# A list schedule's table refitted to corrected durations, with the first q load in two pieces

## The chip, the cores and the metric

The kernel runs on one core of one Trainium2 chip. The metric is the device time of one execution in microseconds, taken as the median of several runs. The engines are named as in the profile: PE multiplies matrices, PEld loads its weights, DVE and ACT work elementwise on 128 partitions, SP issues DMAs, POOL does almost nothing here. ACT issues a few DMAs too (its queue is written ACTq, that of SP is SPq).

## What is computed

Three stages in a row, all in float32. Attention with a threshold (4 batches, 8 heads, 576 positions, head size 64), then a feed-forward layer with softmax and layer norm (2304 tokens, 512 to 1024 to 512), then one with softplus (512 to 2048 to 512):

```python
scores = scale * np.matmul(q, k.transpose(0, 1, 3, 2))
thresh = np.max(scores, axis=-1, keepdims=True) - tau
scores = np.where(scores >= thresh, scores, -1000000000.0)
attn = softmax(scores)            # written out in full in the reference
x = np.matmul(attn, v)            # heads side by side: 2304 x 512
...
h = x @ w_in
solu = h * softmax(h)
ln = (solu - mean(solu)) / np.sqrt(var(solu) + 1e-06) * g_ln
x = ln @ w_out
...
h = x @ w2_in
g = np.maximum(h, 0.0) + np.log1p(np.exp(-np.abs(h)))
out = g @ w2_out
```

## The kernel before

The program is straight-line code: every instruction is written out once. What stands where is decided when the kernel is built, by `Plan`. Each piece of work is an `Op` with an engine, a time that it holds its engine (`occ`), a time until others can use its result (`fin`), what it comes after, what buffers it takes, and a due number. `Plan.order` plays the program through: at each step it takes the engine that can start soonest and on it the ready operation with the least due number. The order that comes out is then emitted, engine by engine, and is fixed; on the chip each engine works through its own list in order and waits on semaphores. The due numbers come from the tables at the top of the file (`JT`, `JA`, `LO`, `LAGS`, `LD`, `JIT`, `PREP` and single numbers), which were fitted. So a wrong duration in an `Op` costs nothing by itself; it gives an order that doesn't suit the chip.

Attention is cut into 44 items, numbered as `n` below. An item is one pair of heads with one or two tiles of 128 queries (or the last 64 queries of two pairs: a tail item, `T`). For each tile PE makes the scores (`s`, line 393; of tail items line 450), DVE takes the maximum (line 349), ACT the exponential (350), DVE masks and sums (352), then come the reciprocals (357, 358) and their spreading (402, 408, 410), PE transposes the weights (368), ACT copies them to SBUF (371), and PE multiplies with v (429). The scores of the next tile need both score buffers back, and these come free with the two exponentials.

Beside this run the weights of the first layer: w_in and w_out come as 64-bit words and are turned into pairs of float32 (ACT 488, DVE 489, 491, 492, then ACT 503 or 500 and DVE 501 or PE 512/513 with ACT 515). The first layer's matmuls on a unit of 256 tokens (line 567; its softmax and norm in lines 584 to 598, its transposes in 610, its second matmul in 627 and 628) are put between the attention work. The second layer (lines 678 and 701) follows; its w_out is loaded and converted in 16 chunks when the first layer has given back its memory: two chunks have been loaded by then, and the third (`raw_out2`) waits for the buffer of the first.

Where the plan sees PE idle for long early in the program it puts filler matmuls there (line 288), which compute nothing that is used.

Of the kernel before, what the change touches and what calls it, by code (L numbers as in the profile page):

```python
# [39 lines left out]
LD = [-11.06, 0.35, 9.2, 14.07, 7.04, 12.77, 7.9, 34.61, 19.66, 38.52, 7.77, 68.68, 10.48, 84.79, 20.67, 17.31, 4.65, 8.82, 1.55, -62.61, -15.71, -19.93, 81.02, 16.74, 91.83, 70.72, 19.84, -5.66, -48.3, 4.79, -22.69, -44.85]  # L40
JIT = [-11.99, -8.79, -5.19, -5.48, 1.8, -10.03, 0.87, -8.03, 6.15, -0.57, 3.09, -24.47, 0.08, 2.59, -34.82, 4.62, 7.64, 16.92, 9.09, 3.38, -14.37, -6.4, -10.15, 3.76, -6.77, -11.43, -14.53, -18.35, -5.02, -26.2, -15.19, -13.01, -2.79, 0.51, -17.2, 8.63, -5.03, -12.19, -11.44, -4.71, -8.08, -1.06, -14.31, -9.49]
YLAG = 4.72
PLOAD = -16.03
W2IN = 60.61
W2OUT = -5.81
TURNED = 4
STICK = 0.48
PREP = [-18.8, -45.68, -12.55, 12.05, 71.4, 119.39, -150.07, 43.1]


def f(ap):
    return ap.bitcast(F32)
# [27 lines left out]
WARM = 130e3  # L80

# [7 lines left out]
class Plan:  # L89
# [17 lines left out]
    def order(self):  # L107
# [12 lines left out]
        mode, dma, done = "", 0, []  # L120
        win, work, slow = 0, {}, False
# [31 lines left out]
        while any(cand.values()):  # L153
# [110 lines left out]
def plan_of(nc, ctx, sb, const, ident, minus, pools, stacks, w1t, x2s, q, k, v, tau, w_in, w_out, g_ln, w2_in, w2_out, out):  # L264
# [5 lines left out]
    plan = Plan(dict(w=W_, s=S_, h2=4, E=NE, T=2, eT=NET, x=2, xr=NXR, xrT=1, q=NPAIR, k=NPAIR, v=NPAIR, ln=3, u=2,  # L270
# [3 lines left out]
    def buf(pool, tag, name, shape, dtype=F32, bufs=1):  # L274
        return Buf(pool, tag, lambda: pools[pool].tile(shape, dtype, tag=tag, name=name, bufs=bufs))
# [23 lines left out]
    o_minus = op("ACT", 200, 300, lambda: act.activation(out=minus, in_=ident, func=AF.Copy, scale=-1.0), after=[o_ident], due=-60)  # L299
    o_table = op("ACT", 1300, 1300, lambda: act.preload_act_table_set("natural_log_exp_and_others"), due=-49.5)  # L300

    def queue(what, i):
        return "ACT" if f"{what}{i}" in ON_ACT else "SP"

    def load_qk(p, due):
# [4 lines left out]
        z["kq"], ql = [], []  # L310
# [3 lines left out]
        for h in range(2):  # L314
            r = slice(64 * h, 64 * h + 64)
            ql.append(load(queue("q", p), lambda r=r: q_.t[r, :], lambda h=h: q[p][:, 640 * h:640 * h + 576], 144, takes=() if h else [q_], uses=[q_] if h else (), due=due))
        z["scaled"] = op("ACT", 574, 678, lambda: act.activation(out=q_.t, in_=q_.t, func=AF.Copy, scale=0.125), after=ql, uses=[q_], due=due + 0.5)
# [37 lines left out]
    def inverse(n, w, sums, masks, due):  # L355
        rv = buf("at", "rinv", f"rinv{n}", [P, 4], bufs=4)
# [20 lines left out]
    def item(n):  # L377
# [4 lines left out]
        sums = buf("at", "sums", f"sums{n}", [P, 4], bufs=4)  # L382
        E = [buf("at", "E", f"E{n}_{i}", [P, 1152], bufs=NE) for i in range(nt)]
        masks = {}
        for kk, i in enumerate(ts):
# [8 lines left out]
            sc = op("PE", 970, 1128, emit_s, after=z["kq"] + [z["scaled"]], takes=s, uses=[z["q"], z["k"]], due=j + JIT[n], mode="R")  # L394
# [7 lines left out]
        o3 = op("ACT", 187 if nt == 1 else 310, 298 if nt == 1 else 410, lambda: act.copy(out=rb.t[:, 0:w, :], in_=rv.t[:, 0:w].unsqueeze(2).to_broadcast([P, w, 64])), after=[o2], takes=[rb], uses=[rv], due=jl + D_SUM)  # L402
# [7 lines left out]
        xc = op("ACT", 162 if nt == 1 else 263, 270 if nt == 1 else 395, lambda: act.copy(out=x.t[:, 0:W], in_=rbk.t[:, 0:W]), after=[rg], uses=[rbk, x], due=jl + D_X)  # L410
# [25 lines left out]
    def tail_item(n):  # L436
# [424 lines left out]
```

## Time and profile before

| what | value |
|---|---|
| median of 3 runs | 912.28 us (912.16 to 912.69) |
| the profiled execution | 914.37 us |
| its span, first to last instruction | 912.6 us |
| PE busy, share of the span | 899.6 us, 99% |
| DVE busy | 690.4 us, 76% |
| ACT busy | 591.1 us, 65% |
| mean granted clock of PE | 0.996 |

The profiled execution took 2.1 us more than the median, and 1.8 us of it lies outside its span. A busy PE is not a PE at its peak, since its matmuls overlap: what can be read is where it is idle, where it runs filler, and the pace from one matmul's start to the next.

### The profile page before, as it was taken

How to read it: one execution, taken by the hardware profiler on the slowest of the kernel's cores; microseconds unless marked ns; L12 is line 12 of the kernel's file. 1: busy time of each engine (PE TensorE's matmuls, PEld its weight loads, DVE VectorE, ACT ScalarE, POOL GpSimd, SP SyncE). 2: the span in 40 equal slices, each digit the busy share in tenths (PEclk: the TensorE clock that was granted, in tenths of full speed). 3: DMA queues.
4: the chain of work that ended last, by engine and by line, in shares of the span. 5: the costliest groups of instructions: out<-in, count | busy, mean ns of one | idle time of the engine just before them, and what ended most of it. 6: DMA issues, size and time to landing. Idle time of an engine off the chain costs nothing.

```text
span 912.6 us, 14433 instructions
## 1 busy us (share of the span) xinstructions
PE 899.6 (99%) x5458; PEld 709.6 (78%) x5458; DVE 690.4 (76%) x1474; ACT 591.1 (65%) x1159; POOL 0.7 (0%) x6
## 2 busy tenths in 40 slices
PE   8999999999999999999999999999999999999998
PEld 6576676677677677788888878888888888888897
DVE  5999898898777778599958969985556555655565
ACT  6978887997778687676757746764444444444454
POOL 0000000000000000000000000000000000000000
PEclk9999999999999999999999999999999999999999
DMA  9405110230231000164414223430021001100010
GB/s 281 161 1 175 54 30 1 84 83 24 66 109 62 2 1 12 59 219 162 139 59 162 93 98 110 135 119 24 1 92 47 1 1 47 47 0 1 1 47 24
DMA packets 32052, 64.63 MB, mean 71 GB/s; under 512 B 3440, under 2 KB 12912, under 8 KB 31984
## 3 DMA queue, kind: packets, MB, share of 16 engines
q1 hardware_dynamic: 31104, 61.62, 20.8%
q10 hardware_dynamic: 880, 2.10, 0.8%
q8 instruction: 43, 0.70, 0.3%
q14 instruction: 25, 0.20, 0.1%
HBM read 49.55 MB, written 14.16 MB: 70 GB/s over the span
## 4 chain that ended last, share of the span: by engine, by line
PE 83%; DVE 7%; ACT 4%; DMA 4%; issue 1%; SPq 1%; ACTq 0%; DVEq 0%
PE w L701 21%; PE h L678 20%; PE w L567 8%; PE w L368 7%; PE w L429 6%; PE s L393 6%; PE w L627 6%; PE w L628 3%; PE w L610 1%; PE w L472 1%; DMA raw<-in_w_in_dram 1%; DVE E L352 1%; DVE nm L349 1%; PE s L450 1%; DMA q<-in_q_dram 1%
## 5 line engine op out<-in xcount | busy, mean ns | idle before, releaser
L678 PE MATMUL h<-x2m,w2h 128*128 128x512 f32 (+1 forms) x640 | 181.6, 368 | 0.0
L678 PEld LDWEIGHTS h<-x2m,w2h 128*128 128x128 f32 x640 | 116.5, 188 | 21.0
L349 DVE TENSOR_REDUCE nm<-s 128x1 f32<-128x576 f32 x144 | 102.7, 752 | 21.7 <-PE s L393 19.1
L678 PE MATMUL h<-x2m,w2l 128*128 128x512 f32 (+1 forms) x320 | 117.7, 368 | 0.0
L701 PE MATMUL w<-wo2h,gh 128*128 128x512 f32 x288 | 112.9, 392 | 1.1 <-ACT wo2h L503 1.1
L701 PE MATMUL w<-wo2l,gh 128*128 128x512 f32 x288 | 113.0, 393 | 0.6 <-DVE wo2l L505 0.6
L352 DVE SCALAR_TENSOR_TENSOR E<-E,etau 128x576 f32<-128x576 f32 x128 | 101.1, 815 | 16.3 <-ACT E L350 14.9
L701 PE MATMUL w<-wo2h,gl 128*128 128x512 f32 x288 | 112.7, 391 | 0.0
L371 ACT COPY eT<-w 128x512 f32<-128x512 f32 (+1 forms) x188 | 92.9, 554 | 19.5 <-PE w L368 18.9
L689 ACT ACTIVATE t<-h 128x512 f32<-128x512 f32 (+1 forms) x80 | 44.3, 554 | 90.9 <-PE h L678 90.9
L627 PE MATMUL w<-lhl,wo1h 128*128 128x512 f32 x288 | 102.8, 397 | 0.0
L350 ACT ACTIVATE E<-s,nm 128x576 f32<-128x576 f32 x128 | 91.6, 756 | 11.2 <-DVE nm L349 11.0
L691 DVE TENSOR_SCALAR gw<-t 128x512 f32<-128x512 f32 (+1 forms) x80 | 31.8, 399 | 80.3 <-ACT t L690 80.1
L693 ACT ACTIVATE gw<-gw 128x512 f32<-128x512 f32 (+1 forms) x80 | 47.1, 589 | 61.1 <-DVE t L692 60.0
L393 PE MATMUL s<-k,q 64*128 64x288 f32 x512 | 83.9, 429 | 2.0 <-ACT E L350 1.4
L628 PE MATMUL w<-lhl,wo1l 128*128 128x256 f32 x288 | 80.7, 280 | 0.0
L429 PE MATMUL w<-eT,v 128*64 128x256 f32 (+1 forms) x720 | 77.8, 364 | 1.6 <-ACT eT L371 1.5
L368 PE MATMUL w<-ident,E 128*128 128x128 f32 x576 | 78.4, 279 | 0.0
L368 PEld LDWEIGHTS w<-ident,E 128*128 128x128 f32 x576 | 63.6, 141 | 17.4 <-issue 6.4
L694 DVE SCALAR_TENSOR_TENSOR gw<-h,gw 128x512 f32<-128x512 f32 (+1 forms) x80 | 51.0, 637 | 33.1 <-ACT gw L693 32.0
L429 PEld LDWEIGHTS w<-eT,v 128*64 128x64 f32 x720 | 47.1, 138 | 28.0 <-ACT eT L371 4.4
L678 PEld LDWEIGHTS h<-x2m,w2l 128*128 128x128 f32 x320 | 60.3, 188 | 10.1
(107 smaller groups left out, 1573.2 us busy)
## 6 DMA issues: line engine op xcount, KB each, us to landing
x2s<-x SPq DMA_DIRECT2D x36, 256.0 KB, 2.0
x2m<-x2s SPq DMA_DIRECT2D x18, 512.0 KB, 6.0
raw_in<-in_w_in_dram SPq DMA_DIRECT2D x16, 512.0 KB, 3.8
raw_out<-in_w_out_dram SPq DMA_DIRECT2D x16, 512.0 KB, 3.6
v<-in_v_dram SPq DMA_DIRECT2D x15, 320.0 KB, 3.4
q<-in_q_dram SPq DMA_DIRECT2D x28, 144.0 KB, 3.6
out_dram<-yo SPq DMA_DIRECT2D x15, 256.0 KB, 2.1
raw<-in_w_out_dram SPq DMA_DIRECT2D x3, 1024.0 KB, 7.8
```

Of the source, the lines that this page charges most:

```text
L349: mx = op("DVE", 668, 750, lambda: dve.tensor_reduce(out=nm.t, in_=src(), axis=AX.XY, op=ALU.max, negate=True), after=[after], takes=[nm], ...
L350: ex = op("ACT", 638, 741, lambda: act.activation(out=dst().rearrange("p (a b) -> p a b", a=2), in_=src(), func=AF.Exp, bias=nm.t, scale=1.0),
L352: return op("DVE", 739, 900, lambda: dve.scalar_tensor_tensor(out=dst(), in0=dst(), scalar=etau, in1=dst(), op0=ALU.is_ge, op1=ALU.mult, a ...
L368: pe.transpose(bk.t[:, P * i:P * i + P], b_.t[:, c:c + P], ident)
L371: copies.append(op("ACT", occ, occ + 111, lambda: act.copy(out=eT.t[:, 0:width], in_=bk.t[:, 0:width]), after=[g], uses=[bk, eT], due=due))
L393: pe.matmul(s[h].t[:, nh, 0:288], z["q"].t[r, c:c + P], z["k"].t[r, 288 * nh:288 * nh + 288], start=True, stop=True)
L429: pe.matmul(o_.t[64 * h:64 * h + 64, 0:W], z["v"].t[:, vcols(c, h)], e[8 if c == 8 else 4 * h + c](), start=(i == 0), stop=(i == 4))
L567: pe.matmul(ps.t, x__[:, part, :], w_[:, part, 512 * n:512 * n + 512], start=(part == 0 and j_ == 0), stop=(part == 3 and j_ == 2))
L627: pe.matmul(o.t.rearrange("p (a q) -> p a q", a=2), w1t["wo1h"][:, c, P * m:P * m + P], lhl.t[:, :, c, :], start=(c == 0), stop=False)
L628: pe.matmul(o.t[:, 0:256], w1t["wo1l"][:, c, P * m:P * m + P], lhl.t[:, 0, c, :], start=False, stop=(c == 7))
L678: pe.matmul(ps.t[:, 0:n], w2t["in", a, c][:, part, :], x.t[:, b_, part, 0:n], start=(part == 0 and j_ == 0), stop=(part == 3 and j_ == 2))
L701: pe.matmul(ys[j].t, g_.t[:, P * j:P * j + P], w2t["out", a, c], start=(c == 0 and i == 0), stop=(c == NC2 - 1 and i == 2))
```

## The change

Five things are changed. Durations of some operations are set anew: ACT's share of the conversions (lines 488, 500, 503), DVE's in line 501, the scaling of the tail items' rows (460, 461), the spreading copies (402, 410). The plan takes the first loads to land later (`FIRST`), and lets PE start at the low clock. The first q load is cut at column 192 of 576, with a scaling for each piece, and the second piece goes through SP. `sums` and `rinv` get eight buffers for four, and the plan is told that there is one `rb`. Two setup operations on ACT change places. Then all fitted tables are new.

```diff
-JT = [0.34, 7.73, 0.9, -3.39, 0.54, ...
+JT = [-0.31, 8.41, -0.42, -4.07, -3.04, ...
...
-AHEAD = dict(PE=0, DVE=0, ACT=0, SP=20, POOL=20, X=20)
+AHEAD = dict(PE=75, DVE=0, ACT=0, SP=35, POOL=20, X=20)
...
-STICK = 0.48
+STICK = 0.03
...
+FIRST = 2500
...
-        mode, dma, done = "", 0, []
-        win, work, slow = 0, {}, False
+        mode, dma, done = "", FIRST, []
+        win, work, slow = 0, {}, True
...
-    o_minus = op("ACT", 200, 300, lambda: act.activation(out=minus, in_=ident, func=AF.Copy, scale=-1.0), after=[o_ident], due=-60)
-    o_table = op("ACT", 1300, 1300, lambda: act.preload_act_table_set("natural_log_exp_and_others"), due=-49.5)
+    o_minus = op("ACT", 200, 300, lambda: act.activation(out=minus, in_=ident, func=AF.Copy, scale=-1.0), after=[o_ident], due=-5)
+    o_table = op("ACT", 1300, 1300, lambda: act.preload_act_table_set("natural_log_exp_and_others"), due=-80)
...
+        cuts = [0, 192, S] if p == 0 else [0, S]
+        z["scaled"] = []
+        for a, e in zip(cuts, cuts[1:]):
...
-        rv = buf("at", "rinv", f"rinv{n}", [P, 4], bufs=4)
+        rv = buf("at", "rinv", f"rinv{n}", [P, 4], bufs=8)
...
-            sc = op("PE", 970, 1128, emit_s, after=z["kq"] + [z["scaled"]], takes=s, uses=[z["q"], z["k"]], due=j + JIT[n], mode="R")
+            sc = op("PE", 970, 1128, emit_s, after=z["kq"] + z["scaled"][0:1 if i == 0 else 2], takes=s, uses=[z["q"], z["k"]], due=j + JIT[n], mode="R")
...
-            t2.append(op("ACT", 590, 695, lambda i=i: act.activation(...), after=[t1[i]], ...))
+            t2.append(op("ACT", 667, 765, lambda i=i: act.activation(...), after=[t1[i]], ...))
...
-        a1 = op("ACT", 100 + 950 * k_, 200 + 960 * k_, ...)
+        a1 = op("ACT", 69 + 1022 * k_, 181 + 1008 * k_, ...)
...
-                h = op("ACT", 525, 620, lambda i=i: act.activation(out=hi()[:, i, :], ...))
+                h = op("ACT", 666, 794, lambda i=i: act.activation(out=hi()[:, i, :], ...))
```

What the tables do to the order is seen in the built programs. Three places are shown, and in all of them the changed program's lines stand seven lower, as its file is longer. ACT at the very start, before the change (`q_101` is the first q, `q_132` the second, `E_0_168` the weights of item 0, `etau` needs the load of tau):

```order
L295 DMA q_101<-in_q_dram 64x576 x2
L299 ACT_TABLE_LOAD
L299 ACTIVATE minus<-ident 128x128
L300 ACT_TABLE_LOAD
L317 ACTIVATE q_101<-q_101 128x576
L734 ACTIVATE etau<-tau_sb 128x1
L317 ACTIVATE q_132<-q_132 128x576
L350 ACTIVATE E_0_168<-s_0_0_139,nm_0_148 128x576
L350 ACTIVATE E_0_168<-s_0_1_140,nm_1_164 128x576
```

And in the changed program (`q_120` is the first q, `q_129` the second):

```order
L301 ACT_TABLE_LOAD
L296 DMA q_120<-in_q_dram 64x192 x2
L300 ACTIVATE minus<-ident 128x128
L741 ACTIVATE etau<-tau_sb 128x1
L324 ACTIVATE q_120<-q_120 128x192
L324 ACTIVATE q_120<-q_120 128x384
L357 ACTIVATE E_0_165<-s_0_0_139,nm_0_148 128x576
L324 ACTIVATE q_129<-q_129 128x576
L357 ACTIVATE E_0_165<-s_0_1_140,nm_1_163 128x576
```

One table load is gone, the other stands ahead of the q load, `etau` ahead of the first scaling, and the scaling of the second q between the two exponentials of item 0. On SP the two DMAs of the first q's second piece stand fourth and fifth, behind k and tau, and the third and fourth k and q now come ahead of the second to fourth v.

PE from the scores of item 6 to those of item 7, before the change (`E4` and `E5` are weights of items 4 and 5):

```order
L393 MATMUL s6_0_0_493<-k2_145,q2_162 128x288
L368 MATMUL w30_503<-ident_81,E4_0_412 128x128 x4
L368 MATMUL w31_514<-ident_81,E4_0_412 128x128 x4
L368 MATMUL w32_521<-ident_81,E4_0_412 128x128
L368 MATMUL w35_524<-ident_81,E5_0_470 128x128 x4
L393 MATMUL s7_0_1_543<-k3_186,q3_203 128x288
```

And the last rows of the same stretch in the changed program:

```order
L436 MATMUL w33_534<-eT4_4_509,v0_137 64x128
L415 MATMUL w29_551<-ident_81,rb4_520 128x128
L375 MATMUL w35_554<-ident_81,E5_0_503 128x128 x4
L375 MATMUL w36_564<-ident_81,E5_0_503 128x128 x4
L375 MATMUL w37_572<-ident_81,E5_0_503 128x128
L519 MATMUL w7_578<-raw1_3_2_275,ident_81 128x512
L520 MATMUL w7_578<-w1h_83,minus_82 128x512
L400 MATMUL s7_0_1_588<-k3_171,q3_182 128x288
```

Between the scores of item 6 and the first of these rows stand eight more of line 436 (item 4's product with v). So item 4's product, ten transposes and a pair for the conversions now lie between the two scores, where thirteen transposes lay.

DVE at the third chunk of the second layer's w_out (`raw_out2`, ending in `wo2l2`), before the change:

```order
L489 TENSOR_SCALAR raw_out2_6385<-raw_out2_6385 128x512
L691 TENSOR_SCALAR gw0_5_6420<-t0_5_6256 128x512
L491 SCALAR_TENSOR_TENSOR raw_out2_6385<-raw_out2_6385 128x512
L489 TENSOR_SCALAR raw_out3_6391<-raw_out3_6391 128x512
L492 SCALAR_TENSOR_TENSOR raw_out2_6385<-raw_out2_6385 128x512
L491 SCALAR_TENSOR_TENSOR raw_out3_6391<-raw_out3_6391 128x512
L697 TENSOR_TENSOR gl0_4_6442<-gw0_4_6243,gh0_4_6432 128x512
L505 TENSOR_TENSOR wo2l2_6323<-raw_out2_6385,wo2h2_6322 128x512
```

And in the changed program:

```order
L496 TENSOR_SCALAR raw_out2_6396<-raw_out2_6396 128x512
L498 SCALAR_TENSOR_TENSOR raw_out2_6396<-raw_out2_6396 128x512
L499 SCALAR_TENSOR_TENSOR raw_out2_6396<-raw_out2_6396 128x512
L496 TENSOR_SCALAR raw_out3_6401<-raw_out3_6401 128x512
L704 TENSOR_TENSOR gl0_3_6439<-gw0_3_6206,gh0_3_6432 128x512
L498 SCALAR_TENSOR_TENSOR raw_out3_6401<-raw_out3_6401 128x512
L512 TENSOR_TENSOR wo2l2_6334<-raw_out2_6396,wo2h2_6333 128x512
```

The chunk's first three steps now follow each other with nothing between them.

## Rows read from the trace of the kernel before

**Rows 1.** Windows: us, busy of PE, PEld, DVE, ACT, POOL (instructions); clock, DMA.

```profile
0.00:25.52 25.52, 21.27 (x172) 17.31 (x172) 15.16 (x31) 17.49 (x32) 0.70 (x6) 1.00 0.94 295
25.52:49.90 24.38, 23.35 (x136) 14.98 (x134) 23.38 (x57) 23.01 (x47) 0.00 (x0) 0.93 0.29 105
49.90:97.90 48.00, 47.00 (x387) 33.48 (x387) 46.58 (x94) 39.44 (x77) 0.00 (x0) 1.00 0.28 84
97.90:120.40 22.50, 22.03 (x176) 15.22 (x175) 19.97 (x50) 20.60 (x44) 0.00 (x0) 1.00 0.26 71
120.40:157.40 37.00, 37.00 (x277) 25.24 (x277) 34.93 (x90) 29.95 (x63) 0.00 (x0) 1.00 0.03 9
157.40:347.50 190.10, 189.45 (x1573) 136.02 (x1571) 155.19 (x360) 149.38 (x305) 0.00 (x0) 1.00 0.17 52
533.90:547.32 13.42, 11.69 (x44) 8.95 (x43) 8.75 (x17) 4.57 (x8) 0.00 (x0) 0.87 0.37 122
```

**Rows 2.** Timeline of ACT and ACTq, first items: start, length, instruction, idle before.

```profile
0.74 1.49 ACTq L295 DMA_DIRECT2D q<-in_q_dram  x2
2.26 1.28 ACT L299 ACT_TABLE_LOAD   x1 [2.26 <-issue]
6.01 0.68 ACT L317 ACTIVATE q<-q 128x576 f32<-128x576 f32 x1 [0.84 <-DMA q<-in_q_dram]
8.77 0.68 ACT L317 ACTIVATE q<-q 128x576 f32<-128x576 f32 x1 [1.99 <-DMA q<-in_q_dram]
12.78 0.28 ACT L402 COPY rb<-rinv 128x128 f32<-128x128 f32 x1
17.23 0.69 ACT L317 ACTIVATE q<-q 128x576 f32<-128x576 f32 x1 [1.07 <-DMA q<-in_q_dram]
```

**Rows 3.** Timeline of SPq, and the landing of tau by tile.

```profile
2.00 0.59 SPq L295 DMA_DIRECT2D tau_sb<-in_tau_dram  x1
3.77 1.24 SPq L295 DMA_DIRECT2D q<-in_q_dram  x2
DMA to landing us min/median/max: 4.1/4.1/4.1
```

**Rows 4.** Timeline of PE, the start.

```profile
1.35 4.92 PE L288 MATMUL w<-ident 128*128 128x128 f32 x28 [1.35 <-POOL ident masks.py:199]
6.74 1.31 PE L393 MATMUL s<-k,q 64*128 64x288 f32 x8 [0.47 <-ACT q L317]
```

**Rows 5.** Timeline of PE around the scores of item 7.

```profile
40.65 1.64 PE L368 MATMUL w<-ident,E 128*128 128x128 f32 x13
43.29 1.87 PE L393 MATMUL s<-k,q 64*128 64x288 f32 x8 [1.00 <-ACT E L350]
```

**Rows 6.** Windows around the two stretches at half clock.

```profile
42.14:45.56 3.42, 2.42 (x15) 1.33 (x15) 3.42 (x11) 3.42 (x9) 0.00 (x0) 1.00 0.00 0
45.56:48.97 3.41, 3.41 (x27) 3.08 (x24) 2.52 (x8) 2.46 (x7) 0.00 (x0) 0.50 0.00 0
543.90:547.32 3.42, 3.42 (x9) 2.65 (x10) 3.42 (x7) 1.45 (x3) 0.00 (x0) 0.50 0.56 169
```

**Rows 7.** The chain that ended last: a run of first-layer matmuls.

```profile
334.80 2.75 PE w L567 x12
```

**Rows 8.** Timeline of PE: transposes between matmuls, and the third chunk's wait.

```profile
508.31 0.39 PE L678 MATMUL h<-x2m,w2l 128*128 128x512 f32 x1
508.55 1.91 PE L610 MATMUL w<-ident,h 128*128 128x128 f32 x16
510.21 0.70 PE L678 MATMUL h<-x2m,w2h 128*128 128x512 f32 x2
...
541.17 0.39 PE L678 MATMUL h<-x2m,w2l 128*128 128x512 f32 x1
542.69 0.50 PE L701 MATMUL w<-wo2h,gh 128*128 128x512 f32 x1 [1.14 <-ACT wo2h L503]
543.79 0.72 PE L701 MATMUL w<-wo2l,gh 128*128 128x512 f32 x1 [0.59 <-DVE wo2l L505]
```

More of the change, by code (lines that the diff above doesn't have):

```diff
@@ L309, in load_qk @@
         k_ = z["k"] = buf("at", "k", f"k{p}", [P, 640], bufs=NPAIR)
[L310 removed]
+        z["kq"] = []
         for h in range(2):
@@ L313, in load_qk @@
             z["kq"].append(load(queue("k", p), lambda r=r, h=h: k_.t[r, 0:576 + 64 * h], lambda h=h: k[p][:, 576 * h:576 + 640 * h], 150, takes=() if h else [k_], uses=[k_] if h else (), due=due))
[L314 to L317, printed above, removed]
+        cuts = [0, 192, S] if p == 0 else [0, S]
+        z["scaled"] = []
+        for a, e in zip(cuts, cuts[1:]):
+            ql = []
+            for h in range(2):
+                r = slice(64 * h, 64 * h + 64)
+                tk = a == h == 0
+                ql.append(load(queue("q", p) if a == 0 else "SP", lambda r=r, a=a, e=e: q_.t[r, a:e], lambda h=h, a=a, e=e: q[p][:, 640 * h + a:640 * h + e], (e - a) / 4, takes=[q_] if tk else (), uses=() if tk else [q_], due=due + (1 if a else 0)))
+            occ = 110 + 0.806 * (e - a)
+            z["scaled"].append(op("ACT", occ, occ + 104, lambda a=a, e=e: act.activation(out=q_.t[:, a:e], in_=q_.t[:, a:e], func=AF.Copy, scale=0.125), after=ql, uses=[q_], due=due + 0.5))
     def load_v(p, due):
@@ L401, in item @@
         rb = buf("at", "rb", f"rb{n}", [P, 4, 64])
-        o3 = op("ACT", 187 if nt == 1 else 310, 298 if nt == 1 else 410, lambda: act.copy(out=rb.t[:, 0:w, :], in_=rv.t[:, 0:w].unsqueeze(2).to_broadcast([P, w, 64])), after=[o2], takes=[rb], uses=[rv], due=jl + D_SUM)
+        o3 = op("ACT", 200 if nt == 1 else 325, 305 if nt == 1 else 416, lambda: act.copy(out=rb.t[:, 0:w, :], in_=rv.t[:, 0:w].unsqueeze(2).to_broadcast([P, w, 64])), after=[o2], takes=[rb], uses=[rv], due=jl + D_SUM)
         rbk = bank()
@@ L409, in item @@
         rg = op("PE", 109 * nt, 109 * nt + 163, emit_r, after=[o3, o_ident], takes=[rbk, x], uses=[rb], due=jl + D_X, mode="T")
-        xc = op("ACT", 162 if nt == 1 else 263, 270 if nt == 1 else 395, lambda: act.copy(out=x.t[:, 0:W], in_=rbk.t[:, 0:W]), after=[rg], uses=[rbk, x], due=jl + D_X)
+        xc = op("ACT", 157 if nt == 1 else 265, 265 if nt == 1 else 390, lambda: act.copy(out=x.t[:, 0:W], in_=rbk.t[:, 0:W]), after=[rg], uses=[rbk, x], due=jl + D_X)
         copies, eTs, e = [], [], {}
@@ L487, in convert @@
         w_ = lambda: lw().bitcast(F32)
[L488 removed]
+        a1 = op("ACT", 69 + 1022 * k_, 181 + 1008 * k_, lambda: act.activation(out=hw().bitcast(F32), in_=hw().bitcast(F32), func=AF.Copy, scale=2.0 ** -112), after=after, uses=[raw], due=due - 0.1)
         a2 = op("DVE", 70 + 535 * k_, 150 + 540 * k_, lambda: dve.tensor_scalar(out=lw(), in0=lw(), scalar1=29, scalar2=None, op0=ALU.logical_shift_right), after=after, uses=[raw], due=due)
@@ L499, in convert @@
             for i in range(2):
-                h = op("ACT", 525, 620, lambda i=i: act.activation(out=hi()[:, i, :], in_=w_()[:, i, :], func=AF.Copy, scale=scale(i)), after=[a4, o_g], uses=[raw], due=due)
-                low.append(op("DVE", 602, 692, lambda i=i: dve.scalar_tensor_tensor(out=lo()[:, i, :], in0=w_()[:, i, :], scalar=scale(i), in1=f(hi()[:, i, :]), op0=ALU.mult, op1=ALU.subtract), after=[h], uses=[raw], due=due))
+                h = op("ACT", 666, 794, lambda i=i: act.activation(out=hi()[:, i, :], in_=w_()[:, i, :], func=AF.Copy, scale=scale(i)), after=[a4, o_g], uses=[raw], due=due)
+                low.append(op("DVE", 665, 752, lambda i=i: dve.scalar_tensor_tensor(out=lo()[:, i, :], in0=w_()[:, i, :], scalar=scale(i), in1=f(hi()[:, i, :]), op0=ALU.mult, op1=ALU.subtract), after=[h], uses=[raw], due=due))
             return low
-        a5 = op("ACT", 100 + 850 * k_, 200 + 850 * k_, lambda: act.copy(out=hi(), in_=w_()), after=[last], uses=[raw], due=due)
+        a5 = op("ACT", 68 + 1004 * k_, 158 + 1018 * k_, lambda: act.copy(out=hi(), in_=w_()), after=[last], uses=[raw], due=due)
         if not turned:
```

49 lines of the change are left out of this document (24 added, 25 removed).

## The prediction, made before the changed kernel was run

> **What bounds the kernel now.** I read the windows first, cut at the scores of certain items, since a share over the whole span mixes stages [rows 1]. Behind 157.40, where the scores of item 20 start, PE is the bound alone: it is idle for 0.65 of the next 190.10 us. Ahead of it PE is idle for 4.25, 1.03, 1.00, 0.47 and 0 us, 6.75 in all, but DVE is nearly as full: 23.38 of 24.38, 46.58 of 48.00, 34.93 of 37.00. So up to item 20 two engines share the bound, and time that PE is spared there counts only as far as DVE can keep up. DVE's busy time up to 157.40 is 15.16 + 23.38 + 46.58 + 19.97 + 34.93 = 140.02. It has nothing to do before the first scores are out, at 6.74 + 1.31 = 8.05 [rows 4]. That leaves it 9.3 us of idle time, the reserve of this part.
>
> Then the timeline of PE, for its waits. The largest early one stands ahead of item 7's scores: 1.00 us until the exponential of an earlier item gives its buffer back [rows 5]. It costs more than itself: PE was busy for 2.42 of 3.42 us there, and in the next 3.41 us the granted clock is 0.50, the lower level of 1.2 GHz [rows 6]. Work at half pace for 3.41 us is 1.7 us lost. The same pair stands at the third chunk of the second layer's w_out: the matmul that should start at 541.17 + 0.23 starts at 542.69, the next, due 0.23 later, at 543.79, and then come 3.42 us at half clock [rows 6, 8]. That is 1.29 + 0.87 + 1.7 = 3.9 us.
>
> **The start.** Before, the first scaling waits for q's landing until 6.01 and takes 0.68; PE follows at 6.74 [rows 2, 4]. A piece of 192 columns should take between the 0.28 of a 128-column copy and 0.68, by its width 0.34. That brings 0.34. But `etau` now stands ahead of it and needs tau, issued at 2.00 and landed 4.1 later, at 6.1 [rows 3]: 0.1 past the old start of the scaling. If tau lands as before, PE starts at about 6.6; two thirds of the first q no longer lie ahead of it, so it may land earlier, and 5.9 is the least I would believe. I take 6.3, a gain of 0.4.
>
> The second item doesn't gain. The second q's DMAs stand two issues later on SP, each 0.62 [rows 3], so its scaling, which waited for the landing until 8.77 [rows 2], starts between 8.77 and 10.0, and the second exponential of item 0 is queued behind it on ACT; the next scores wait for that exponential. What comes back is the fourth q: ACT waited 1.07 us for it at 17.23 [rows 2], and it is loaded ahead of three v now. The table load that goes (1.28 [rows 2]) lay in a stretch where ACT waited for q anyway: nothing. The extra scaling and the two extra DMAs cost engines with room: nothing, but for the order on SP just told. I found no wait that the extra buffers of `sums` and `rinv` would end by themselves; they enter through the order.
>
> **Up to item 20.** The two orders can be counted up to item 20's first scores. DVE has exactly the same instructions in both. PE has 75 first-layer matmuls for 90, and four fillers more (33 for 29 in all). So 15 matmuls of 2.75 / 12 = 0.229 [rows 7], 3.4 us of work, move behind item 20, where they are paid in full. Item 20 must come 3.4 us sooner just to break even. How much sooner it comes is DVE's matter. Where DVE was pressed hardest, from 25.52 to 97.90, it was idle for 2.42 of 72.38 us, 3.3% [rows 1]; this share over the whole 149 us gives 5.0 us of idle for the 9.3, so 4.3 sooner, and 0.4 more for the earlier start. Net: 3.4 - 4.7 = -1.3. Bounds: with DVE's idle time unchanged +3.0; with most of PE's waits gone, as far as DVE allows, some -4. What speaks for the middle is that covers are where waits were: ahead of item 7's scores 13 transposes (1.64 [rows 5]) become a product with v, ten transposes and a conversion pair, more than the missing 1.00; less first-layer work also means that nothing else of PE must be hurried in between.
>
> **Changes of kind.** Counted in the orders, PE goes from one kind of work to another 298 times for 277: ten more times from matmuls to transposes, ten more back, and one. Going in costs next to nothing (0.24 from 508.31 to 508.55 [rows 8]); coming back, two matmuls take 0.70 where 0.23 + 0.39 would do, 0.08. Ten of these are 0.8; I take +0.7, and as bounds 0 and 2 (0.1 for each).
>
> **The third chunk.** In the changed order 63 matmuls for 60 lie between the last matmul of the first layer and the first that needs this chunk: 3 x 0.23 = 0.7 of cover. DVE's steps on the chunk have nothing between them now, which lets ACT's part come some 0.3 sooner. The wait of 1.29 falls to about 0.3. The 0.87 behind it hangs on `wo2l2`, which still has work of the next chunk and a `gl` ahead of it: it stays. So -0.9, and I count the half-clock stretch as gone in half of the cases, -0.8. Together -1.7, bounds -3.9 and 0.
>
> **Sum.** -1.3 + 0.7 - 1.7 = -2.3 us: a span of 910.3 for 912.6. The profiled execution took 914.37, 2.1 above the median; on the median's scale 912.28 - 2.3 = 910.0. A change within 0.2%, 1.8 us, can't be told from none here.
>
> **A rule against the start.** By the timeline ACT's queue issued both q DMAs from 0.74 to 2.23, and the table load began behind them at 2.26 [rows 2]. Now the load stands first; if it held the issue up, q would leave 1.28 later. Perfetto Trace Analysis of the Trainium skill (section Sequencer Loop) says that a sequencer pushes an instruction for its engine into a queue and reads on, with rare exceptions; by that the DMAs leave at once. No row of before has a load ahead of a DMA. DMA: Bandwidth & Descriptors of the Trainium skill (section Issuing engines are not separate DMA queues) says that all issuers share the same 16 engines, and that issuing from several saves only the time of issuing; by that the smaller first piece helps through fewer bytes ahead, not through its queue. Without any gain at the start the sum is -1.9.
>
> **Rivals.**
> *The waits move.* DVE's idle time falls to about 7 only, since each scores' wait is traded for another further on. Then item 20 comes 2.3 + 0.4 sooner, net +0.7; with +0.7 and -1.7 the sum is -0.3: 912.0. For it speaks that half of DVE's idle time lies ahead of 25.52 and behind 97.90, where it waits for others' chains, and these chains are as long as before.
>
> *Too little left for PE early, too much late.* The 15 matmuls are lost to the part where PE had time for them, and DVE, the co-bound, comes no sooner. Item 20 then starts at 157.0, net +3.0; +3.0 + 0.7 - 1.7 = +2.0: 914.3. It decides from the point where item 20 comes less than 0.6 us sooner than 157.40 (+2.8 net, +1.8 in all). For it: 34.93 of 37.00 us between items 16 and 20, where PE didn't wait at all. Against it: 4.25 us of idle PE ahead of 25.52, with reloads now in a better order.
>
> *The table load holds q.* The first scores come at 7.1 for 6.3, +0.8 on any of the three, 910.8 on the forecast. I give it 0.15, across the others.
>
> **Chances.** The forecast 0.50, moved waits 0.32, the late rest 0.18. The likeliest case alone reaches from 907 to 910.4. For eight times in ten I go from 906.8 (both half-clock stretches and most waits gone) to 914.0, most of the way to the slow rival. Faster by over 0.2% 0.50, within it 0.32, slower 0.18.
>
> **What will show it.** First scores between 5.9 and 6.6, with `etau` just ahead of the scaling; at 7 or later the table load held q. The scores of item 20 at 152 to 154, with DVE idle for 4 to 6 us up to there; at 156 or later the slow rival is right. No wait ahead of item 7's scores and a granted clock of 1.00 around them. A wait below half a microsecond at the first matmul of the third chunk, and one of nearly 0.9 at the second. The forecast is wrong if new waits of PE behind item 20 exceed a microsecond, for I have none there.

## The result and the profile after

The changed kernel takes 917.43 us in the median of 4 executions (915.87 to 920.56), the kernel before 912.22 beside it: a ratio of 1.0063 (95% interval 1.0035 to 1.0090), slower. On a second chip, with 12 executions, it was 915.30 for 912.44, 1.0027 (1.0006 to 1.0048). The prediction had 910.0, with a range from 906.8 to 914.0. The profiled execution took 920.56, with a span of 918.6 us.

The windows first, cut at the scores of items 4, 8, 13, 14, 16, 20 and 43 of the changed kernel, as in [rows 1], and last the stretch from the first matmul with the second layer's w_out to the first with its third chunk:

```profile
0.00:25.96 25.96, 20.56 (x163) 17.02 (x163) 13.51 (x30) 15.02 (x30) 0.70 (x6) 1.00 0.84 272
25.96:50.43 24.47, 24.25 (x176) 16.04 (x175) 24.47 (x55) 24.30 (x47) 0.00 (x0) 1.00 0.33 124
50.43:89.48 39.05, 38.63 (x325) 26.89 (x324) 36.64 (x81) 32.64 (x67) 0.00 (x0) 1.00 0.31 98
89.48:104.66 15.18, 9.89 (x69) 6.99 (x67) 10.48 (x19) 8.44 (x15) 0.00 (x0) 0.89 0.32 94
104.66:122.79 18.13, 18.13 (x150) 12.94 (x149) 17.69 (x35) 17.46 (x35) 0.00 (x0) 1.00 0.13 37
122.79:159.27 36.48, 35.98 (x257) 24.54 (x256) 35.89 (x101) 31.43 (x67) 0.00 (x0) 1.00 0.00 1
159.27:375.63 216.36, 215.93 (x1725) 158.50 (x1723) 164.08 (x391) 160.11 (x331) 0.00 (x0) 1.00 0.16 50
544.27:549.71 5.44, 5.44 (x25) 4.50 (x24) 4.13 (x8) 2.47 (x5) 0.00 (x0) 1.00 0.25 102
```

Item 13 comes at 89.48, 8.4 us ahead of the 97.90 of before: the new order was well ahead. In the next window PE, DVE and ACT all stand: PE is busy for 9.89 of 15.18 us, and its clock averages 0.89. Item 14 comes 3.0 us later than before (104.66 for 101.70), and item 20 1.9 later. The timeline shows what the three stood for:

```profile
81.95 0.75 DVE L508 SCALAR_TENSOR_TENSOR wo1l<-raw,g_sb,wo1h 128x512 fp32r<-128x512 f32 x1 [0.30 <-ACT wo1h L507]
82.72 0.38 SPq L296 DMA_DIRECT2D raw<-in_w_out_dram  x1
82.75 0.45 ACTq L296 DMA_DIRECT2D raw<-in_w_out_dram  x1
...
90.61 1.09 PE L375 MATMUL w<-ident,E 128*128 128x128 f32 x8
...
93.97 2.21 ACT L495 ACTIVATE raw<-raw 128x1024 f32<-128x1024 f32 x2 [5.56 <-DMA raw<-in_w_out_dram]
94.04 0.69 DVE L496 TENSOR_SCALAR raw<-raw 128x1024 uint32<-128x1024 uint32 x1 [5.44 <-DMA raw<-in_w_out_dram]
...
94.65 0.81 DVE L359 SCALAR_TENSOR_TENSOR E<-E,etau 128x576 f32<-128x576 f32 x1
...
95.38 1.22 DVE L498 SCALAR_TENSOR_TENSOR raw<-raw 128x1024 uint32<-128x1024 uint32 x1
...
96.52 0.42 DVE L439 TENSOR_TENSOR xr<-w,x 128x256 f32<-128x256 f32 x1
...
96.99 1.12 PE L375 MATMUL w<-ident,E 128*128 128x128 f32 x4 [5.29 <-DVE xr L439]
```

The first layer's w_out is loaded in four quarters of 1 MB, and the third and fourth go into the memory of the first two (`lhl`, one buffer). So both wait for the last step on the second quarter, DVE's at 81.95. Then they leave at the same moment, one on SP's queue and one on ACT's, and both land 11 us later: the tile's landing row, over both loads, reads

```profile
DMA to landing us min/median/max: 11.0/11.1/11.2
```

The first steps of the third quarter stand at the head of both ACT's and DVE's lists. Behind them on DVE are a mask, a second conversion step, and the `xr` that gives PE its PSUM bank (memory for its results) back. PE stands for 5.29 us, and then runs 3.42 us at half clock (a granted clock of 0.50, the lower level of 1.2 GHz):

```profile
96.47:99.89 3.42, 2.90 (x12) 2.50 (x12) 3.42 (x6) 1.96 (x5) 0.00 (x0) 0.50 0.17 52
```

Before, the third quarter left at 71.24 and the fourth at 74.52, behind six loads of k and q on SP; they landed at 77.57 and 82.66, and no engine waited more than a microsecond for them:

```profile
71.24 0.44 ACTq L295 DMA_DIRECT2D raw<-in_w_out_dram  x1
74.52 0.53 SPq L295 DMA_DIRECT2D raw<-in_w_out_dram  x1
77.59 0.70 DVE L489 TENSOR_SCALAR raw<-raw 128x1024 uint32<-128x1024 uint32 x1 [0.99 <-DMA raw<-in_w_out_dram]
```

The start: the table load (0.73) and the q issues (0.77) go side by side, `etau` has its tau at 5.07, and the first scores come at 5.57 for 6.74 [rows 4].

```profile
0.73 1.28 ACT L301 ACT_TABLE_LOAD   x1 [0.73 <-PEq L858]
0.77 1.47 ACTq L296 DMA_DIRECT2D q<-in_q_dram  x2
5.07 0.20 ACT L741 ACTIVATE etau<-tau_sb 128x1 f32<-128x1 f32 x1 [2.47 <-DMA tau_sb<-in_tau_dram]
5.57 1.31 PE L400 MATMUL s<-k,q 64*128 64x288 f32 x8 [0.32 <-ACT q L324]
...
23.70 1.19 ACT L495 ACTIVATE raw<-raw 128x1024 f32<-128x1024 f32 x1 [2.10 <-DMA raw<-in_w_in_dram]
24.76 0.28 ACT L417 COPY x<-w 128x128 f32<-128x128 f32 x1
25.09 0.94 PE L289 MATMUL w<-ident 128*128 128x128 f32 x6 [2.06 <-ACT x L417]
```

The gain is gone well before item 4. ACT stands for the third q until 12.62, which in the kernel before had landed by 12.19, and PE stands behind ACT; the third scores come at 15.37 for 13.91. The first two lines are of the changed kernel, the last of the kernel before:

```profile
12.62 0.68 ACT L324 ACTIVATE q<-q 128x576 f32<-128x576 f32 x1 [1.97 <-DMA q<-in_q_dram]
13.54 0.33 PE L415 MATMUL w<-ident,rb 128*128 128x128 f32 x1 [1.60 <-ACT rb L409]
...
12.19 0.68 ACT L317 ACTIVATE q<-q 128x576 f32<-128x576 f32 x1 [1.47 <-DMA q<-in_q_dram]
```

Item 4 comes at 25.96 for 25.52, and then w_in is late too: it is issued at 13.99 for 13.00 and lands at 23.7 for 19.7, ACT stands at its first step, and PE behind ACT for 2.06 us.

Behind item 20 the third chunk's wait is gone altogether: in the last window above PE is busy throughout, at full clock. But PE has three new waits:

```profile
396.14 1.06 PE L617 MATMUL w<-ident,h 128*128 128x128 f32 x8 [1.43 <-DVE h L605]
...
517.05 1.07 PE L617 MATMUL w<-ident,h 128*128 128x128 f32 x8 [1.52 <-DVE h L605]
...
606.43 0.50 PE L685 MATMUL h<-x2m,w2h 128*128 128x512 f32 x1 [0.69 <-DVE gw L701]
```

### The profile page after: what moved, and what is told of

Read it like the earlier page. It is cut to its first block, busy times and chain, and to the rows that moved or that the text cites. A ratio compares the mean times of both kernels' runs of the same rounds, so it can differ in the third digit from the quotient of the medians.

```text
span 918.6 us, 14415 instructions
## 1 busy us (share of the span) xinstructions
PE 898.8 (98%) x5466; PEld 709.0 (77%) x5466; DVE 689.8 (75%) x1474; ACT 587.3 (64%) x1159; POOL 0.7 (0%) x6
## 4 chain that ended last, share of the span: by engine, by line
PE 77%; DVE 11%; DMA 4%; ACT 3%; issue 2%; SPq 1%; DVEq 0%; ACTq 0%
PE w L708 18%; PE h L685 18%; PE w L574 10%; PE w L375 7%; PE s L400 6%; PE w L436 6%; PE w L634 6%; PE w L635 3%; SPq L296 1%; PE w L617 1%; DMA raw_in<-in_w_in_dram 1%; DMA raw<-in_w_out_dram 1%; PE w L479 1%; DVE E L359 1%; DVE nm L356 1%
## 5 line engine op out<-in xcount | busy, mean ns | idle before, releaser
L704 DVE TENSOR_TENSOR gl<-gw,gh 128x512 fp32r<-128x512 f32 (+1 forms) x80 | 50.9, 636 | 71.1 <-ACT gh L703 70.7
L703 ACT CAST gh<-gw 128x512 fp32r<-128x512 f32 (+1 forms) x80 | 46.1, 576 | 69.2 <-PE w L708 61.3
```

## Experiments

All but the one on the kernel before are the changed kernel with one or two edits. Where operations are put elsewhere, the plan is the same and only the place of the named ones in the written-out lists moves (`LATE`: the number of an operation, and ns by which it stands later in the order; 103 and 112 are the two loads, 99 to 102 the last steps on the second quarter, 104 to 120 the steps on the third and fourth). The ratios are to the kernel before on the same chip, from 12 executions to its 35, with their 95% intervals. They are not the quotients of the medians (a0's medians give 1.0031). The medians of before on the three chips are 912.31 (e1 to e4), 912.44 (a0, e5, e6, b1) and 912.90 (f1 to f4), so that runs of different chips are compared by their ratios; an interval is about 0.15 to 0.2% to either side.

| run | median us | ratio (interval) | third, fourth quarter land, us from issue | PE's wait for them |
|---|---|---|---|---|
| a0, changed again | 915.30 | 1.0027 (1.0006 to 1.0048) | 10.4, 10.3 | 4.52 |
| e1, one queue | 912.09 | 0.9988 (0.9971 to 1.0004) | not read | not read |
| e5, one queue again | 912.22 | 0.9989 (0.9968 to 1.0009) | 5.0, 7.1 | none |
| f1, both on ACT | 913.50 | 0.9999 (0.9984 to 1.0014) | 7.8, 10.0 | 1.46 |
| e2, conversions later | 915.14 | 1.0024 (1.0009 to 1.0038) | 9.8, 9.6 | none |
| e4, loads earlier | 914.20 | 1.0015 (1.0000 to 1.0030) | 7.6, 6.7 | none |
| e6, one queue, earlier | 913.98 | 1.0013 (0.9995 to 1.0032) | 4.9, 7.9 | none |
| b1, before, one queue | 912.38 | 0.9993 (0.9971 to 1.0014) | 5.7, 8.1 (issued 3.6 apart) | no new one |
| e3, q whole | 914.22 | 1.0017 (1.0001 to 1.0033) | 7.8, 7.6 | 1.85 |
| f2, one queue, q whole | 911.44 | 0.9981 (0.9964 to 0.9998) | 7.5, 9.7 | 1.60 |
| f3, second piece on ACT | 911.72 | 0.9985 (0.9969 to 1.0000) | 5.0, 7.1 | none |
| f4, f2 and norm first | 912.05 | 0.9979 (0.9964 to 0.9994) | 6.9, 9.0 | 0.97 |

**The two quarters on one queue (e1, e5).**

```diff
-        e = sp if eng == "SP" else act
+        e = sp if eng == "SP" or kb == 1024 else act
```

> The changed kernel with one edit: the third quarter of the first layer's w_out is issued on SP, just ahead of the fourth, instead of on ACT's queue at the same moment. In the changed kernel both were issued at 82.7 and landed at 93.7 and 93.9, and PE then stood for 5.29 us. Theory 'pair': two loads of 1 MB on two queues share the DMA engines, so that the first lands with the second. On one queue the third quarter lands some 3 us ahead of the fourth (8 us behind its issue), PE's wait falls from 5.3 to about 2.5, and the median from 917.4 to about 914.5. Rival 'slow engines': the DMA engines were simply slow there, both land late again, and the wait and the median stay (within 1 us).

The median is 912.09, 2.4 us below what the theory had. The one execution that was profiled took 3.1 ms and shows nothing of the others, so the kernel was run and profiled once more (e5), beside the changed kernel itself (a0):

> The same kernel as the first run with one queue (912.09), for a profile that is not disturbed: that run's profiled execution took 3.1 ms. Theory 'pair': the third quarter lands 2.5 to 3.5 us ahead of the fourth, PE's wait there is below 2.5 us and its clock stays at 1.00; item 20 comes at 153 to 156, the median is 911 to 913. Rival: both land together again, and the gain has its place elsewhere in the trace.

> The changed kernel as it is, timed beside the others on one chip. Its one profile had an unusually late landing of both w_out quarters (11 us behind the issue; in the run with q whole it was 7.6) and of w_in (23.7 for 22.2 to 22.4 in three runs with the same start). Theory 'pair': the wait for the quarters is there in each execution, 2 to 5 us with the clock behind it, and the median is 914.5 to 917, clear of before. Rival 'one bad chip': the 917.43 was a matter of that chip, and the median here is within 1 us of before's.

912.22 again, and 915.30 for the changed kernel on the same chip: this one edit is worth 3.1 us. About half of that goes with the clock: of a0's 12 executions 8 have a mean clock below 0.999, of e5's one, and the others have medians of 913.72 and 912.20. The wait is in a0's profile too (4.52, and 3.4 us at half clock), so it was not a bad chip. In e5's windows, cut at items 4, 8, 13, 14, 16 and 20, the stretch from item 13 to 14 takes 8.72 us for 15.18, and DVE is busy throughout; item 20 comes at 152.51:

```profile
0.00:25.61 25.61, 21.53 (x163) 17.56 (x163) 13.51 (x30) 14.95 (x30) 0.70 (x6) 1.00 0.82 268
25.61:50.07 24.46, 24.25 (x175) 16.06 (x175) 24.46 (x55) 24.30 (x47) 0.00 (x0) 1.00 0.35 132
50.07:89.12 39.05, 38.63 (x324) 26.89 (x324) 37.53 (x83) 33.70 (x68) 0.00 (x0) 1.00 0.31 102
89.12:97.84 8.72, 8.68 (x69) 5.82 (x67) 8.72 (x16) 7.31 (x15) 0.00 (x0) 1.00 0.52 145
97.84:116.03 18.19, 18.19 (x151) 13.02 (x149) 18.19 (x37) 17.14 (x35) 0.00 (x0) 1.00 0.13 37
116.03:152.51 36.48, 35.98 (x257) 24.55 (x256) 35.95 (x101) 31.43 (x67) 0.00 (x0) 1.00 0.01 1
```

Issued one behind the other at 82.37, the quarters land 5.0 and 7.1 us later, and the first step starts at 87.94 without a wait of its own:

```profile
82.37 0.89 SPq L296 DMA_DIRECT2D raw<-in_w_out_dram  x2
...
87.94 1.21 ACT L495 ACTIVATE raw<-raw 128x1024 f32<-128x1024 f32 x1
88.15 0.70 DVE L496 TENSOR_SCALAR raw<-raw 128x1024 uint32<-128x1024 uint32 x1
```

**Which queue (f1).** The fourth quarter's load is issued on ACT's queue as well, right behind the third's.

```diff
-        ld = load(queue("w", i), ..., due=due - PLOAD)
+        ld = load(queue("w", i), ..., due=due - PLOAD); ld.fn = ld.fn if i != 7 else lambda: act.dma_start(...)
```

> The changed kernel with both last quarters of w_out issued on ACT's queue, one behind the other, where one quarter was on ACT's and one on SP's. Theory 'pair': what costs is that two queues share the DMA engines, so that the first quarter lands with the second; one queue serves them in turn, whichever queue it is. The third quarter lands 5 to 6 us behind its issue and 2 to 3 us ahead of the fourth, PE has no wait over 1 us there, and the median is 911.5 to 913, as with both on SP (912.09 and 912.22). Rival 'ACT's queue': loads issued by ACT are served worse; the third quarter lands 8 us or more behind its issue, PE waits over 1.5 us, and the median is 914 or more.

One queue serves them in turn here too: the third quarter lands 2.6 us ahead of the fourth. But both were late in the profiled execution, and the wait is 1.46, between the two theories' bounds:

```profile
80.85 0.41 ACTq L296 DMA_DIRECT2D raw<-in_w_out_dram  x1
...
81.30 0.48 ACTq L538 DMA_DIRECT2D raw<-in_w_out_dram  x1
...
91.75 0.66 PE L375 MATMUL w<-ident,E 128*128 128x128 f32 x4 [1.46 <-DVE xr L439]
```

The median is 913.50 where before has 912.90 on this chip, a ratio 0.0011 above e5's, within the intervals. SP's queue gave 7.5 and 9.7 on the same chip in f2, so a late landing is no mark of ACT's queue. Over all profiles of the changed order, on two queues (5 of them) the third quarter landed up to 0.9 us after the fourth, 7.6 to 11.2 behind its issue; on one queue (6) 2.5 to 3.4 ahead of it, 4.9 to 7.8 behind its issue.

Within each kind the spread has another cause, a last part of the load that lags (last section). Without such a lag the third quarter took 7.6 to 7.8 us on two queues (e3, e4) and 4.9 to 5.0 on one (e5, e6, f3); with it 9.8 to 11.2 (the first profile, e2, a0) and 6.9 to 7.8 (f1, f2, f4). So the 5.29 us of the first profile are the pair and a lag together: the pair alone gave 1.85 (e3), a lag alone 0.97 to 1.60 (f4, f1, f2), and without either PE did not wait (e5, f3). One profile of each kernel doesn't tell how often the lag is there; that the pair costs time on the median is shown by e5 against a0 and, with q whole, by f2 against e3 (0.9981 for 1.0017).

**The work put elsewhere (e2, e4).**

```diff
-FIRST = 2500
+FIRST, LATE = 2500, {n: 5500 for n in range(104, 121) if n != 112}
...
-        for o in sorted(done, key=lambda o: o.start):
+        for o in sorted(done, key=lambda o: o.start + LATE.get(o.n, 0)):
```

> The changed kernel with all steps of the conversion of the last two quarters of w_out put 5.5 us later in the order, so that ACT and DVE have other work ahead of them while the loads are under way; PE's order is the same. Theory 'pair': the loss up to item 20 is this wait and the half clock behind it (5.3 + 1.7). Item 14's scores come at 97 to 99 for 104.7, item 20's at 152 to 154 for 159.3, and the median falls by 4 to 7 us, to 911 to 913. Rival 'order at large': the moved first-layer matmuls and the conversions' own work hold PE up at the next places; item 20 comes at 157 or later, and the median stays above 915.

The wait goes, and item 14 comes at 96.55, even sooner than the theory has it. But item 20 comes at 155.55, between the two theories, and the median of 915.14 is the rival's. The conversions press on the exponentials and reciprocals of items 14 and 15, and PE waits for these:

```profile
101.99 1.23 PE L400 MATMUL s<-k,q 64*128 64x288 f32 x6 [0.38 <-ACT E L357]
...
105.06 1.32 PE L375 MATMUL w<-ident,T 128*128 128x128 f32 x8 [0.94 <-ACT T L468]
```

e4 has the same second edit with

```diff
+FIRST, LATE = 2500, {99: -6100, 100: -6200, 101: -9100, 102: -8900, 103: -9300, 112: -9300}
```

> The changed kernel with the last four steps of the second quarter of w_out put 6 to 9 us earlier on ACT and DVE, so that their buffer comes free and the loads of the last two quarters start some 9 us sooner; the conversions behind them stay where they were. Theory 'pair': the loads land by 84 to 87, ahead of their first steps, the wait of 5.3 goes, item 20's scores come at 152 to 154 and the median falls to 911 to 913, as in the run with later conversions. Rival 'order at large': the four steps now press on the exponentials and maxima that follow (2.9 us of DVE and ACT), and item 20 comes at 157 or later, the median above 915.

Item 20 comes at 153.18 and no wait for the quarters is left, as the theory has it; but the median is 914.20, 1.2 above its bounds, and the profiled execution was the fastest of the twelve. The moved steps cost something of their own: PE waits 0.58 and 0.56 at two places (until 71.96 and 82.85) where e5 has no wait. The first is for a copy on ACT, whose list has one of the moved steps just ahead of it. The second is for another load: ACT stands 1.81 us for a q issued at 75.61, while the two quarters were under way, and PE stands behind ACT. So the rival was right in part for both: in e2 the wait was bought with DVE's and ACT's time in a part where these are full, in e4 partly with the lateness of the next load.

**Both edits, and the edit in the kernel before (e6, b1).**

> Both at once: the two quarters on SP, and their buffer freed 6 to 9 us sooner. Theory 'pair': either edit takes the wait, so that both together give little more than the better one: item 20 at 152 to 154, median 910.5 to 912.5. Rival 'two queues cost more than this wait' (the runs so far: 912.09 with one queue and a wait left, 914.20 with two queues and no wait): the second queue slows the loads of every execution, and this kernel beats the one with earlier loads by 2 us or more.

> The kernel before with the same edit: the third quarter goes through SP, behind one k load. There the two quarters were issued 3.3 us apart and landed 5.1 us apart, and no engine stood for them longer than 1 us. Theory 'pair': nothing to gain, the median stays within 1 us of before's. Rival 'two queues cost more than this wait': faster by 1.5 us or more here too.

e6 (913.98) is not better than e4 (914.20) and worse than e5, 1.5 us above what was expected; in it ACT stands 2.24 us for the same q, and PE 0.92 behind ACT. The edit does nothing in b1 (912.38 for 912.44). So a second queue costs nothing by itself that could be measured here. It costs where two loads leave together and the first one's user stands next in line.

**The first q (e3, f2, f3).** In e3 the pieces stay in the plan, but the first load and scaling take all 576 columns, and the second write nothing:

```diff
-            ql.append(load(..., lambda r=r, a=a, e=e: q_.t[r, a:e], lambda h=h, a=a, e=e: q[p][:, 640 * h + a:640 * h + e], ...))
+            ql.append(load(..., lambda r=r: q_.t[r, :], lambda h=h: q[p][:, 640 * h:640 * h + S], ...)); ql[-1].fn = (lambda: None) if a else ql[-1].fn
```

> The changed kernel with the first q loaded and scaled in one piece again (two DMAs on SP and one scaling fewer), all else in the same order. Theory 'issues': the split brings the first scores 1.2 us sooner (5.57 for 6.74), but its two more issues on SP (1.2 us) and its narrower rows bring w_in later (23.7 for 19.7), for which ACT and PE wait 2.06 us behind 22.75. Then the first scores come at about 6.6, w_in lands by 22.5, the wait falls below 1.2, and the median stays within 1 us of 917.4. Rival 'head start': the 1.2 us of the start carry through; the wait behind 22.75 stays at 2, and the median rises by about 1 us.

> Both quarters on SP, and the first q in one piece again. Theory 'issues': the split gives 1.2 us at the first scores and loses it again by item 5, since its two more issues bring w_in later; in the run with q whole alone item 5 came at 34.63, for 35.6 to 36.7 with the split. Then the median is 910.5 to 912, 0.5 to 1.5 below that with the split (912.1). Rival 'head start': the start's 1.2 us hold, and the median is 913 or more.

f2 is e3 with the first edit. In f3 the second piece is kept and issued on ACT (`e = act if kb == 96 else ...`, and `LATE = {8: 100}`, which puts it behind the first):

> Both quarters on SP, the first q in two pieces, but its second piece issued on ACT's queue behind the first, so that SP's list is two issues shorter, as it was before the change. Theory 'issues': w_in is issued 1.1 us sooner on SP, at 12.9 for 14.0, and lands by 22; item 5 comes at 35 or sooner, the median is 911 to 912, and the start's gain is kept (first scores by 6.0). Rival 'narrow rows': it is the number of bytes in a row that slows the first loads; w_in lands at 22 to 23.5 as with the second piece on SP, and the median stays at 912.1 within 0.5.

In e3 the wait for w_in goes and the first scores fall back, as the theory has it; the median of 914.22 has to be held against a0's 915.30, not the 917.43 of another chip. With q whole the first scores come at 6.90 to 7.13, w_in is issued at 12.9 to 13.5 and lands at 19.5 to 21.1, and PE has no wait for it. Yet item 5 comes at 34.6 to 36.1, with the split at 35.2 to 37.0. f3 issues w_in at 13.66, which lands at 21.8. The medians (ratios 0.9981, 0.9985, and 0.9988 and 0.9989 for the split with one queue) can't be told apart. So the 1.2 us of the first scores end in no time either way. The place is the third q: ACT gets it at 12.46 in e3 and at 12.62 in the first profile, and the third scores come at 15.21 and 15.37, whatever the start was. Whether issues or narrow rows delay w_in stays open; in the first profile a lag was part of it (15 of the 16 parts of its first load had landed by 22.13, the last at 23.68).

**One of the late waits (f4).** f2 with `LATE = {1823: 1540, 1388: 830}`: DVE's last steps of a norm (603, 604, 605) go ahead of a 605 and a 439 that nothing waits for yet.

> As the run with both quarters on SP and q whole, and with DVE's last three steps of a layer norm put ahead of two steps that nothing waits for yet, at the place where PE stood 1.43 us in every profile of the changed order (394.3 in the first). Theory: this wait is one of the changed order's own, in DVE's list; it falls to 0.4 or less, and the median by 1.0 against the run without this edit, to about 910. Rival: the wait moves on to the next matmuls, which need what these transposes give, and the median stays.

```profile
389.43 1.07 PE L617 MATMUL w<-ident,h 128*128 128x128 f32 x8 [0.51 <-DVE h L605]
```

The wait falls from 1.44 in f2's profile to 0.51. The median doesn't follow (912.05 for 911.44), and the last first-layer matmul starts at 489.96 for 489.75, though item 20 came 0.7 sooner than in f2; f4 has waits of 0.52 (until 245.91) and 0.48 (until 412.39) that f2 lacks. So in these profiles what was saved had been lost again by then, as the rival has it, if not all at the next matmuls. The medians can't decide: a gain of 1.0 lies within the intervals, and both profiled executions were the slowest of their twelve. The ratios of f4 and f2, 0.9979 and 0.9981, are the only ones clear of 1 on the fast side: by them these versions are faster than the kernel before by 1.9 and 1.7 us, by the medians by 0.9 and 1.5.

## Why the prediction was wrong

**The step that failed** is the one that carried DVE's idle share over to the time of item 20: "this share over the whole 149 us gives 5.0 us of idle for the 9.3, so 4.3 sooner". DVE's busy time up to item 20 is 13.51 + 24.47 + 36.64 + 10.48 + 17.69 + 35.89 = 138.7, so it was idle for 159.3 - 6.9 - 138.7 = 13.7 us behind the first scores, where the step had 5.0, and 5.44 of it in one wait for the third quarter. I had followed the conversions as instructions of DVE, found the same ones in both orders, and did not follow the two loads behind them: when their buffer comes free, on which queues they leave, and who stands at the head of the lists when they land. With the two on one queue and nothing else changed (e5), item 20 comes at 152.51, where I had 152.7. That is luck in part: DVE was idle for 152.5 - 7.2 - 138.4 = 6.9 us behind the first scores, not 5.0, about what the rival of moved waits had (7). What made up for it is that DVE was busy for 138.4 us, not 140.0. The instructions up to item 20 were not quite the same: the profile of before has three steps of line 598 there, e5's only two of the same step (line 605), 0.81 us each.

**A rule that was there.** In all profiles of the changed order with the quarters on two queues they landed within a microsecond of each other, on one queue 2.5 us apart or more. DMA: Bandwidth & Descriptors of the Trainium skill (section Queues, rings and completion order) says that each DMA engine goes round robin between the queues that it has work for, packet by packet. The traces agree: at the end of the two loads of the first profile their packets of 4 KB start in turn, those of ACT's queue at 91.93, 92.24 and 92.55, those of SP's at 92.08 and 92.39, each queue's 0.31 us apart; on one queue (f2) they start 0.155 apart. I had taken from that page only that issuers share the engines.

**The sum, closed.** Against the profiled execution of before, e5 is 910.3 - 912.6 = -2.3, the sum that I forecast, but from other terms. Item 20: -4.9 (forecast -4.7). The 15 matmuls behind it: +3.4, as forecast and not measured apart. The third chunk: -3.9 (forecast -1.7). New waits of PE behind item 20: +2.4 (0.70, 1.44 and 0.22) for 0.4 in before, +2.0 (forecast 0). That leaves +1.1 for changes of kind and all else (forecast +0.7).

**The level.** Even that -2.3 was not there to be had on the median: e5's is 912.22 for 912.44. The profiled execution of before was one of its slower ones: it had two stretches at half clock. In the first batch of runs the kernel before had a mean clock of 0.999 or 1.000 in 22 of 35 executions, with a median of 911.77, and less in 13, with 915.07. At which places the slower ones lost their clock is not on record. I scaled the level to the median but took the gains from the profile; what a stretch at half clock costs in a third of the executions is no gain on their median. Against b1's profile, of full clock (span 909.3, item 20 at 156.12, third chunk 0.52 + 0.87), the same terms (0.7 for changes of kind) give -3.6 + 3.4 - 1.4 + 2.0 + 0.7 = +1.1, and e5's span is 1.0 longer.

**Point by point.** The start: the first scores came even sooner than forecast (5.57 in the profile, 5.5 to 5.9 in the runs with the split, for 6.3), since tau landed 1.1 sooner than before, with fewer bytes of q ahead of it (with q whole, in e3, `etau` starts at 6.07 again); the table load held nothing, so that rival fell. That the extra DMAs cost "nothing, but for the order on SP just told" was wrong: w_in left 1.0 later and landed 1.7 to 3.9 later, for up to 2.1 us of PE's time, by profile; and the 0.4 that I had carried from the start to item 20 was gone at the third scores. Item 7: no wait worth the name (0.12) and full clock, as said, though it came at 46.46 for 43.29. The third chunk: the wait went, for a reason that I had not named (last section). "I have none there", of PE's waits behind item 20: wrong, 1.43 + 1.52 + 0.69. That term stood at nothing without a count of what DVE's lists would do there, and by the prediction's own words over a microsecond makes it wrong; in e5 it was 2.4 us. The slow rival stood nearest to the measured time for another reason: its condition, item 20 less than 0.6 us sooner for want of DVE's time, does not hold once the quarters are on one queue.

## What to carry to other kernels

When an order is moved, follow every load whose buffer is given back by a moved instruction: its issue, what leaves beside it on other queues, and which engine has its first user at the head of its list. Two loads that leave together and are needed one after the other were served better on one queue here (5.0 us for 7.8, without a lag). And a gain on a wait that a profile shows counts on the median only if most executions have that wait; the mean clocks of the timed executions tell how often its half-clock stretch is there.

## What was not expected of the hardware

**A lagging last part.** In the changed kernel the DMA engines are full from 84 to about 89.5, and then a tenth or two of them work for 2 us and more; in e5 the same bytes end at 89.3 with next to no tail. The views are of 82.7 to 94 and of 82.3 to 93, in 40 slices, with the share in tenths:

```profile
DMA  2697996979899898999999984112111039596989
```

```profile
DMA  4675999799999999999989999700000000357959
```

The tail is no matter of two queues. f2, on one, has it too, from 88.9 to 91.7, and there it is too thin for the row of shares; the row of rates shows it, at 30 GB/s where the bulk has 400 (82 to 93 in 40 slices):

```profile
GB/s 103 121 93 186 326 419 250 277 343 387 402 417 357 432 402 387 372 432 402 417 417 402 417 432 402 104 30 30 30 15 30 30 30 74 164 311 154 205 295 239
```

The trace counts a load's landing in 16 parts, and what waits for the load starts with the last. Of f2's third quarter 15 parts had landed by 87.18 and the last at 89.54; of a0's, on two queues, 15 by 89.98 and the last at 92.92; of e5's, without a tail, 15 by 87.32 and the last at 87.36. Why a last part lags in six of the eleven profiles of the changed order was not tried, and stays open.

**Instruction loads and the third chunk.** Before, the third chunk left at 533.64 and landed 5.85 us later; in the changed kernel it landed 3.47 us behind its issue at 541.71, and PE took it up at 549.71. Its high and low half were converted at 548.74 and 549.54, 1.0 and 0.4 us ahead of their matmuls: without the 2.4 us of the landing PE would have waited again. So DVE's order, on which I had built that term, is not what made the difference. In the stretch of before (533.6 to 541.6) the queue of instruction loads has one packet; its share of 1.9% of 16 engines for 8.0 us is 2.4 us of one engine, and behind the bulk there is a tail again:

```profile
DMA  0000095997899879989631112000100010000000
...
q8 instruction: 1, 0.02, 1.9%
```

In the changed kernel (541.7 to 549.7) there is no such packet, and no tail:

```profile
DMA  0000084598999999998321000000000000000000
```

b1, which has such a packet of 1.0 us at this place, had its chunk land after 5.1 us and waited 0.52 for it. All eleven profiles of the changed order have none beside this load, and it landed 3.4 to 3.6 us behind its issue. And before lost its time in one part: 15 of the 16 had landed 3.39 us behind the issue, the last 2.46 later, as long as the packet took (in b1 15 by 3.54, the last 1.55 later, for a packet of 1.0). Runtime: NRT & Kernel Launch of the Trainium skill (section Instruction fetch mechanics) says that instructions are fetched in blocks of 16 KB over a DMA queue of the engine's own, and that the cost of this is mostly hidden; here the packet's size agrees, and a load beside it was late. That the packet is the cause is read from the profiles and wasn't tried.
